# Fused adaLN, cached attention and token mixer at decode: epilogue pieces at two places of each round, and a tail with other engines

## The chip, the cores and the metric

The kernel runs on one NeuronCore of one Trainium2 chip. The metric is the device time of one execution in microseconds; shown are the median of the runs and, from one profiled execution, a trace. The engines are PE (TensorE: matrix products; PEld is its weight load), DVE (VectorE), ACT (ScalarE: activations from a table that has to be loaded), POOL (GpSimd) and SP (SyncE, which here only issues DMAs). Each engine works through its own instructions in the order in which they were written and waits on semaphores for the others.

## The reference

Four rows (B = 4) of width D = 512 go through an adaLN-conditioned block: attention with 32 query heads on 8 cached key/value heads of 4096 positions and 128 channels, and then a token-mixing MLP whose hidden width is F = 1792 (there is one token, so each of the 512 channels goes through the same small MLP 1 to 1792 to 1).

```python
mod = (_silu(c) @ w_mod).reshape(c.shape[0], 6, 1, -1)
sa, ca, ga, sb, cb, gb = (mod[:, 0], ..., mod[:, 5])
h = _layernorm(x, axis=-1) * (1 + ca) + sa
x = x + ga * _A_ref(h, A_k_cache, A_v_cache, A_wq, A_wo)
h = _layernorm(x, axis=-1) * (1 + cb) + sb
x = x + gb * _B_ref(h, B_w1, B_b1, B_w2, B_b2)

# _A_ref: p = softmax(q k^T / sqrt(128)); o = p v; return o @ wo
# _B_ref: h = layernorm(x); u = gelu(h * w1 + b1); return u @ w2 + b2
```

All is float32. The key and value caches are 2 x 32 tiles of 2 MB (one for each row and kv head), and w_q, w_o and w_mod add some 22 MB.

## The kernel before

A *round* i (0 to 31) is one pair of row b = i // 8 and kv head h = i % 8. The main loop runs rounds 0 to 27; rounds 28 to 31 are written out after it (the tail), and `finish` ends the last row. Five 2 MB buffers (`ring`) take K and V tiles in turn; SP issues each load when the buffer it takes has been read. The order on each engine is the order of the program: nothing is rescheduled.

One pass of the loop, number i, does in this order: the scores of round i + 2 (PE, L215) and their row maximum m (DVE, L218); the first half of the projection of round i - 1 (`project_a`, PE L292, then oT on DVE, L294); the transposes of the exponentials of round i + 1 (PE L245; copied to pT on DVE, L251); the second half of the projection (`project_b`, L303 or L310, added to acc on DVE, L319); `colmax` (PE L224, DVE L226) and `expo` (PE pb L233, DVE nm L235, ACT p L238, an Exp) of round i + 2, with the first half of the values product of round i (`values`, L267) between the two; the second half of the values; and the copy po of their result (DVE, L271).

When all 8 heads of row b are done, the *epilogue* of row b runs piece by piece in the eight rounds of the next row. `epilogue` (L394) is a generator, and the loop calls it after the second half of the values (L515 to L519), one piece a round and two in the fifth: (0) fold of the projections, residual and statistics; (1) adaLN (`gather`, `adaln`); (2) the second layernorm (`gather`, `bcast`, `affine`, whose hb is made by ACT at L374), and the first two *pairs*. A pair is two of the 14 blocks of the hidden width: `expand` makes it on DVE (L380), a Gelu activates it in place on ACT (L409, seven pairs to a row), and `contract` or, for rows 0 and 1, `contract_wide` reduces it on PE (L385, L391) into py. Then follow (3) contraction of pairs 0 and 1, pairs 2 and 3 made; (4) contraction of 2 and 3, pairs 4 and 5 made; (5) their contraction, pair 6 made; (6) its contraction, and ZK = py + b2 on DVE (L439). A pair is always contracted in a later piece than the one that made it, and a later round.

Row 2's epilogue runs in the loop only in rounds 24 to 27; its later pieces are called in the tail (L540, L551, L557) and in `finish` (L450, L452).

For the last row the attention gate is multiplied into the last two heads' output weights ahead of time: `spread_gate` makes the gate as a 128x512 tile, `fold_gate` (L487) multiplies it into eight 128x512 blocks of `wo` on DVE (L490). Four are done at the end of round 24 and four at the end of round 25 (L530). Round 30 projects with blocks 0 to 3, round 31 with 4 to 7.

`finish` (L442) has the last row's statistics, `modmm(pg, 5)` (the product for gb, 32 PE instructions, L200), adaLN, the remaining two pieces of row 2's epilogue, the second layernorm, and the last row's 14 blocks (DVE expansions L380, ACT L460 and L465, PE L385). After the expansions DVE multiplies rows 0 to 2 by gb and adds the residual (L467, L468), copies gb (L470), SP stores the three rows (L473), DVE finishes the last row (L474, L475), and ACT's queue stores it (L476).

Of the kernel before, what the change touches and what calls it, by code (L numbers as in the profile page):

```python
# [19 lines left out]
P = 128  # L20
# [11 lines left out]
def adaln_decode(ctx: ExitStack, tc: tile.TileContext, small, x, wmod, wq, kT, v, wo, out):  # L32
# [161 lines left out]
        if i == NS - 1:  # L194
            load_wm(5)

    def modmm(pm, t):
        for k in range(4):
            for c in range(4):
                mm(pm[32 * c:32 * c + 32, :], sT8[:, k].rearrange("p b r -> p (b r)"),  # L200
                   WM[t][:, k, c * P:(c + 1) * P], start=(k == 0), stop=(k == 3))
# [150 lines left out]
    def adaln(b, pst):  # L352
        mean, var = norm(pst)
        a = wk.tile([P, P], F32, name="a")
        h1 = wk.tile([P, P], F32, name="h1")
        r = rsqrt(var, P, "e", lambda: dv.scalar_tensor_tensor(
            a, XK[:, b], mean, prep[:, 3], op0=OP.subtract, op1=OP.mult))
        dv.scalar_tensor_tensor(h1, a, r, prep[:, 2], op0=OP.mult, op1=OP.add)
        return h1, stats(h1, b)

    def bcast(h1, b, pb=None):
        if pb is None:
            pb = ps_e.tile([P, 4, P], F32, name="phb", tag="e")
        for c in range(4):
            e = 32 * c + 8 * b
            mm(pb[:, c, :], ident[:, e:e + 1].to_broadcast([P, P]), h1, start=True, stop=True)
        return pb.rearrange("p c n -> p (c n)")

    def affine(pst, pb):
        mean, var = norm(pst)  # L370
        hb = wk.tile([P, D], F32, name="hb")
        wr = wk.tile([P, NF], F32, name="wr")

        nc.scalar.activation(hb, pb, AF.Identity, bias=mean, scale=-1.0)  # L374
        rsqrt(var, P, "e", out=wr, times=w1n)
        return hb, wr

    def expand(u, hb, wr, js):
        for e, j in enumerate(js):
            dv.tensor_scalar(u[:, e, :], hb, wr[:, j:j + 1], b1[:, j:j + 1], op0=OP.mult, op1=OP.add)  # L380
# [13 lines left out]
    def epilogue(b):  # L394
        residual(XK[:, b], fold_groups(ps_e, ACC.pop(b), "e"))
        stm = stats(XK[:, b], b)
        yield
        h1, stm = adaln(b, gather(stm))
        yield
        pst = gather(stm)  # L400
        hb, wr = affine(pst, bcast(h1, b))
        done = []

        def activate(*pairs):
            for j2 in pairs:
                js = (2 * j2, 2 * j2 + 1)
                u = up.tile([P, 2, D], F32, name="u")
                expand(u, hb, wr, js)
                nc.scalar.activation(u, u, AF.Gelu_apprx_tanh)  # L409
                done.append((u, js))  # L410

        activate(0, 1)
        yield
        wide = b < B - 2
        py = ps_e.tile([P, D if wide else P], F32, name="py", tag="e")

        def consume():
            while done:
                (contract_wide if wide else contract)(py, *done.pop(0))

        consume()
        activate(2, 3)
        yield
        consume()
        yield
        activate(4, 5)
        yield
        if wide:
            consume()
        activate(6)  # L430
        yield
        consume()
        if wide:
            yw = wk.tile([P, D], F32, name="yw", tag="yw", bufs=1)
            dv.tensor_copy(yw, py)
            py = fold_groups(ps_e, yw, "e")
        else:
            yield
        dv.tensor_scalar(ZK[:, b], py, b2, None, op0=OP.add)  # L439
        yield  # L440

    def finish(b, pg, xp, epi):  # L442
        uu = [ring.tile([P, 8, D], F32, name=f"uu{i}", tag="kv") for i in range(2)]
        U = [uu[j // 8][:, j % 8] for j in range(NF)]
        stm = stats(xp, b)
        dv.tensor_copy(XK[:, b], xp)
        pst = gather(stm)
        modmm(pg, 5)
        h1, stm = adaln(b, pst)
        next(epi)  # L450
        pst = gather(stm)
        next(epi)  # L452
        py = ps_s.tile([P, 8, P], F32, name="py3", tag="s")
        pb = bcast(h1, b, py[:, 4:])
        py = py[:, 0]
        hb, wr = affine(pst, pb)
        for js in ((0,), (1,), (2, 3), (4, 5), (6, 7), (8, 9), (10, 11), (12,), (13,)):
            j = js[0]
            if j < 2:
                nc.scalar.activation(U[j], hb, AF.Gelu_apprx_tanh, bias=b1[:, j:j + 1], scale=wr[:, j:j + 1])  # L460
                u = U[j].unsqueeze(1)
            else:
                u = uu[j // 8][:, j % 8:j % 8 + len(js)]
                expand(u, hb, wr, js)
                nc.scalar.activation(u, u, AF.Gelu_apprx_tanh)  # L465
            contract(py, u, js)
        dv.tensor_mul(osb[:, :B - 1], ZK, pg.unsqueeze(1).to_broadcast([P, B - 1, P]))  # L467
        dv.tensor_add(osb[:, :B - 1], osb[:, :B - 1], XK[:, :B - 1])  # L468
        gbl = cst.tile([P, P], F32, name="gbl")
        dv.tensor_copy(gbl, pg)  # L470
        dst = out.rearrange("b (c n) -> b c n", c=4)
        for e in range(B - 1):
            nc.sync.dma_start(dst[e], osb[8 * e:P:32, e])  # L473
        dv.scalar_tensor_tensor(osb[:, b], py, b2, gbl, op0=OP.add, op1=OP.mult)  # L474
        dv.tensor_add(osb[:, b], osb[:, b], XK[:, b])  # L475
        nc.scalar.dma_start(dst[b], osb[8 * b:P:32, b])  # L476

    def spread_gate():
        pgb = ps_m.tile([P, 4, P], F32, name="pgb", tag="m")
# [7 lines left out]
    def fold_gate(gate, es):  # L487
        for e in es:
            w = wo_t[HKV - 2 + e // REP][:, e % REP]
            dv.tensor_mul(w, w, gate)  # L490
# [6 lines left out]
        colmax(i)  # L497
        expo(i)
    transposes(0)
    epi = iter(())  # L500
    for i in range(NS - 4):
        load_k(i + 3)
        if i == NS - 5:
            load_k(NS - 1)
        load_v(i + 1)
        scores(i + 2)
        if i:
            project_a(i - 1)
        transposes(i + 1)
        if i:  # L510
            project_b(i - 1)
        colmax(i + 2)
        values(i, range(8))
        expo(i + 2)
        values(i, range(8, 16))  # L515
        if i and i % HKV == 0:
            epi = epilogue(i // HKV - 1)
        for _ in range((1, 1, 1, 1, 2, 1, 1, 0)[i % HKV]):
            next(epi, None)  # L519
        if 3 <= i <= 5:  # L520
            t = i - 1
            pm = mod(t)
            dst = prep[:, {2: 1, 3: 2, 4: 3}[t]]
            if t == 4:
# [5 lines left out]
        if i == NS - HKV or i == NS - HKV + 1:  # L530
            e = 4 * (i - NS + HKV)
            fold_gate(gate, range(e, e + 4))
    n = NS - 4
    load_v(n + 1)
    scores(n + 2)
# [1 line left out]
    transposes(n + 1)  # L537
    project_b(n - 1)
    colmax(n + 2)
    next(epi)  # L540
    expo(n + 2)
    scores(n + 3)
    transposes(n + 2)
    colmax(n + 3)
    expo(n + 3)
    values(n, range(16))
    load_v(n + 2)
    transposes(n + 3)
# [12 lines left out]
    values(n + 2, range(8, 16))  # L561
# [8 lines left out]
    mm(x3, ident, ep, start=False, stop=False)  # L570
    project_a(n + 3)
    project_b(n + 3, x3)
    finish(B - 1, pgx[:, 0], x3, epi)


# [29 lines left out]
```

## Time and profile before

| | |
|---|---|
| time, median of 3 runs | 392.44 us (392.14 to 392.52) |
| profiled execution | 395.09 us, of which the span of the trace is 393.3 us |
| mean granted TensorE clock | 0.904 |
| PE busy | 298.7 us (76%) |
| DVE busy | 180.7 us (46%) |
| ACT busy | 99.3 us (25%) |
| POOL busy | 0.7 us |
| HBM read | 157.32 MB, 400 GB/s over the span |

The times in the trace are microseconds from the start of the span. A row of the timeline has the start, the duration, the engine, the line of the kernel, the operation, the tiles (out<-in), the shapes and how many instructions were merged; in brackets stands how long the engine had been idle and what ended that. In the chain of waits a row has start, duration and the engine's work or transfer that the end of the kernel hung on.

### The profile page before, as it was taken

Reading aid. Unit: us, or ns where it says so; the run is one execution under the profiler, and the core shown is the slowest. Engines: PE = TensorE matmul, PEld = TensorE weight load, DVE = VectorE, ACT = ScalarE, POOL = GpSimd, SP = SyncE. Lnnn points to the kernel's source line nnn. Section 1 sums busy time; section 2 is a strip of 40 time slices with the busy share of each in tenths; the row PEclk is TensorE's granted clock in tenths of the full one; section 3 lists DMA queues with packets and bytes.
Section 4 is the critical chain, followed back from the end, with each engine's and each line's share of the span. In section 5 each row is a group of like instructions: output and inputs, shape, how many; then the busy total and the mean of one; then the engine's idle time right before and its main releaser. Section 6 shows DMA issues by size and latency. Waiting matters only on the chain.

```text
span 393.3 us, 7322 instructions
## 1 busy us (share of the span) xinstructions
PE 298.7 (76%) x3180; PEld 151.6 (39%) x3180; DVE 180.7 (46%) x491; ACT 99.3 (25%) x122; POOL 0.7 (0%) x6
## 2 busy tenths in 40 slices
PE   0576694837767478998788789888888777998976
PEld 0112342304324133453333345443334344565663
DVE  1522342304413232677454425675545357564465
ACT  1001211101101110116653202156541101474325
POOL 0000000000000000000000000000000000000000
PEclk9999588859969785999999969999999969899996
DMA  8999999999999999999999999999999999999600
GB/s 324 427 428 427 435 423 441 427 420 433 425 431 427 437 432 427 428 430 428 435 424 433 427 428 432 432 429 427 427 437 432 425 433 425 432 424 422 275 2 3
DMA packets 12711, 157.80 MB, mean 401 GB/s; under 512 B 1524, under 2 KB 1540, under 8 KB 1928
## 3 DMA queue, kind: packets, MB, share of 16 engines
q1 hardware_dynamic: 12672, 157.34, 94.1%
q8 instruction: 25, 0.41, 0.4%
q14 instruction: 6, 0.05, 0.0%
q10 hardware_dynamic: 8, 0.00, 0.0%
HBM read 157.32 MB, written 0.01 MB: 400 GB/s over the span
## 4 chain that ended last, share of the span: by engine, by line
DMA 53%; PE 35%; DVE 9%; ACT 1%; issue 1%; SPq 0%; DVEq 0%
DMA k<-in_kT 39%; DMA v<-in_v 12%; PE s L215 9%; PE pv L267 6%; PE s L245 3%; PE s L135 2%; PE py L385 2%; PE pq L310 2%; DMA sm<-in_small 2%; PE qs L150 2%; PE pt L292 2%; PE pa L303 2%; DVE m L218 2%; PE pb L233 1%; DVE mx L226 1%
## 5 line engine op out<-in xcount | busy, mean ns | idle before, releaser
L215 PE MATMUL s<-k,QT 128*32 128x512 f32 x512 | 73.8, 701 | 52.0 <-DMA k<-in_kT 51.7
L238 ACT ACTIVATE p<-s,nm 128x1024 f32<-128x1024 f32 x32 | 35.7, 1115 | 215.0 <-DVE nm L235 214.9
L218 DVE TENSOR_REDUCE m<-s 128x1 f32<-128x1024 f32 x32 | 39.2, 1224 | 90.8 <-PE s L215 90.7
L267 PE MATMUL pv<-v,pT 128*32 128x256 f32 x960 | 65.1, 390 | 5.0 <-DMA v<-in_v 4.8
L215 PEld LDWEIGHTS s<-k,QT 128*32 128x32 f32 x512 | 14.8, 119 | 86.9 <-DMA k<-in_kT 62.0
L245 PE MATMUL s<-ident,p 128*128 128x128 f32 x256 | 37.9, 296 | 0.0
L267 PEld LDWEIGHTS pv<-v,pT 128*32 128x32 f32 x960 | 26.8, 110 | 20.4 <-PE pm L224 5.3
L245 PEld LDWEIGHTS s<-ident,p 128*128 128x128 f32 x256 | 33.0, 162 | 2.3 <-ACT p L238 1.3
L292 PEld LDWEIGHTS pt<-sel,po 128*128 128x128 f32 x126 | 18.3, 209 | 30.7 <-issue 21.5
L303 PE MATMUL pa<-wo,oT 128*32 128x512 f32 x192 | 27.3, 642 | 0.0
L271 DVE COPY po<-pv 128x256 f32<-128x256 f32 x30 | 12.7, 425 | 26.3 <-PE pv L267 26.3
L409 ACT ACTIVATE u<-u 128x1024 f32<-128x1024 f32 x21 | 21.2, 1051 | 4.5 <-DVE u L380 4.4
L226 DVE TENSOR_REDUCE mx<-pm 1x128 f32<-1x512 f32 x32 | 21.5, 672 | 0.8 <-PE pm L224 0.8
L292 PE MATMUL pt<-sel,po 128*128 128x4 f32 x126 | 21.0, 272 | 0.5 <-DVE po L271 0.5
L380 DVE TENSOR_SCALAR u<-hb,wr,sm 128x512 f32<-128x512 f32 x42 | 20.2, 542 | 0.4
L319 DVE TENSOR_TENSOR acc<-acc,pa 128x512 f32<-128x512 f32 x21 | 14.4, 688 | 11.4 <-PE pa L303 11.4
L135 PE MATMUL s<-wm,sT 128*4 128x512 f32 x16 | 8.7, 702 | 14.0 <-DVE sT L121 14.0
L238 ACT ACT_TABLE_LOAD x10 | 12.8, 1283 | 19.7 <-DVE nm L235 19.6
L233 PEld LDWEIGHTS pb<-neg,mx 1*128 1x128 f32 x64 | 9.8, 190 | 17.3 <-DVE mx L226 16.1
L233 PE MATMUL pb<-neg,mx 1*128 1x1 f32 x64 | 12.5, 262 | 3.8 <-DVE mx L226 3.6
L409 ACT ACT_TABLE_LOAD x11 | 14.1, 1283 | 4.3 <-DVE u L380 4.2
L251 DVE COPY pT<-s 128x128 f32<-128x128 f32 x31 | 9.0, 291 | 11.5 <-PE s L245 11.0
(136 smaller groups left out, 229.5 us busy)
## 6 DMA issues: line engine op xcount, KB each, us to landing
k<-in_kT SPq DMA_DIRECT2D x32, 2048.0 KB, 21.8
v<-in_v SPq DMA_DIRECT2D x29, 2048.0 KB, 22.8
wq<-in_wq SPq DMA_DIRECT2D x4, 2048.0 KB, 17.7
wo<-in_wo SPq DMA_DIRECT2D x8, 1024.0 KB, 22.3
v<-in_v SPq DMA_DIRECT2D x5, 1024.0 KB, 15.6
wm<-in_wmod SPq DMA_DIRECT2D x2, 2048.0 KB
wm<-in_wmod SPq DMA_DIRECT2D x2, 1024.0 KB, 14.7
v<-in_v SPq DMA_DIRECT2D x1, 512.0 KB, 17.9
```

Source lines behind the costliest of these rows:

```text
L135: mm(s0[0:B, t * D:(t + 1) * D], sT[:, k, :], wm01[:, t, k, :], start=(k == 0), stop=(k == 3))
L215: mm(s[32 * c:32 * c + 32, n * 512:(n + 1) * 512], QT[:, b, h, :], KT[i][:, (n * 4 + c) * 512:(n * 4 + c + 1) * 512], start=True, stop=True)
L218: dv.tensor_reduce(m, s, axis=AX.X, op=OP.max)
L226: dv.tensor_reduce(mx, pm.rearrange("o (c r) -> o r c", c=4).unsqueeze(1).to_broadcast([1, 4, 32, 4]), axis=AX.X, op=OP.max)
L233: mm(pb, mx.rearrange("o c r -> o (c r)"), neg1, start=True, stop=True)
L238: nc.scalar.activation(p, s, AF.Exp, bias=nm, accum_out=l)
L245: nc.tensor.transpose(pt[:, k, :], p[:, k * P:(k + 1) * P], ident)
L267: mm(pv[32 * q:32 * q + 32, :], pTs[i % 3][:, k, :], VT[i][:, k * 2:(k + 1) * 2, :].rearrange("p j d -> p (j d)"), start=(k < 4), stop=(k ...
L292: mm(pt, po[:, c * DH:(c + 1) * DH], sel[:, c * REP:(c + 1) * REP], start=(c == 0), stop=(c == n - 1))
L303: mm(pa[32 * g:32 * g + 32, :], oT[:, g:g + 1].to_broadcast([P, 32]), wo_t[h][:, g, :], start=True, stop=True)
L380: dv.tensor_scalar(u[:, e, :], hb, wr[:, j:j + 1], b1[:, j:j + 1], op0=OP.mult, op1=OP.add)
L409: nc.scalar.activation(u, u, AF.Gelu_apprx_tanh)
```

## The change

The generator becomes a class `Mixer` whose pieces are called at two places of each round: the *inner* place, between `expo` and the second half of the values, and the *outer* place, where the generator was called. Residual, adaLN and second layernorm go to the inner place of the first three rounds of a row; pairs are made one by one, 0 at the outer place of the third round, then one at the inner and one at the outer place of the next rounds; at the outer place of rounds four to seven all pairs that are done are contracted, ahead of the new pair. ZK is made by ACT for row 2.

The gate products are spread: blocks 0 and 1 in round 24, 2 and 3 after the values of round 28, 4 and 5 around those of round 29, 6 and 7 after the projection of round 29. In the tail, pairs 3 to 6 of row 2 are made one at a time. In `finish` the gb product is split (k = 0 ahead of adaLN, k = 1 to 3 behind the broadcast), gb is copied before the last row's expansions, rows 0 to 2 are multiplied and added on GpSimd from that copy and stored by SP, and the last row's store is issued by SP too.

```diff
-    def modmm(pm, t):
-        for k in range(4):
+    def modmm(pm, t, ks=range(4)):
+        for k in ks:
...
+    class Mixer:
...
+        def inner(self, k):
+            if k == 0:
+                self.residual()
+            elif k == 1:
+                self.modulate()
+            elif k == 2:
+                self.normalise()
+            elif k <= 5:
+                self.both()
+
+        def outer(self, k):
+            if 3 <= k <= 6:
+                self.consume()
+            if 2 <= k <= 5:
+                self.both()
+            if k == 6:
+                self.close()
...
-        modmm(pg, 5)
+        modmm(pg, 5, (0,))
         h1, stm = adaln(b, pst)
-        next(epi)
+        mix.consume()
+        mix.close()
         pst = gather(stm)
-        next(epi)
         py = ps_s.tile([P, 8, P], F32, name="py3", tag="s")
         pb = bcast(h1, b, py[:, 4:])
         py = py[:, 0]
+        modmm(pg, 5, (1, 2, 3))
         hb, wr = affine(pst, pb)
+        gbl = cst.tile([P, P], F32, name="gbl")
+        dv.tensor_copy(gbl, pg)
+        po = nc.gpsimd
+        po.tensor_mul(osb[:, :B - 1], ZK, gbl.unsqueeze(1).to_broadcast([P, B - 1, P]))
+        po.tensor_add(osb[:, :B - 1], osb[:, :B - 1], XK[:, :B - 1])
+        dst = out.rearrange("b (c n) -> b c n", c=4)
+        for e in range(B - 1):
+            nc.sync.dma_start(dst[e], osb[8 * e:P:32, e])
...
-        dv.tensor_mul(osb[:, :B - 1], ZK, pg.unsqueeze(1).to_broadcast([P, B - 1, P]))
-        dv.tensor_add(osb[:, :B - 1], osb[:, :B - 1], XK[:, :B - 1])
-        gbl = cst.tile([P, P], F32, name="gbl")
-        dv.tensor_copy(gbl, pg)
-        dst = out.rearrange("b (c n) -> b c n", c=4)
-        for e in range(B - 1):
-            nc.sync.dma_start(dst[e], osb[8 * e:P:32, e])
         dv.scalar_tensor_tensor(osb[:, b], py, b2, gbl, op0=OP.add, op1=OP.mult)
         dv.tensor_add(osb[:, b], osb[:, b], XK[:, b])
-        nc.scalar.dma_start(dst[b], osb[8 * b:P:32, b])
+        nc.sync.dma_start(dst[b], osb[8 * b:P:32, b])
...
         expo(i + 2)
+        if i and i % HKV == 0:
+            mix = Mixer(i // HKV - 1)
+        if mix:
+            mix.inner(i % HKV)
+            if i == NS - HKV:
+                fold_gate(gate, (0, 1))
         values(i, range(8, 16))
-        if i and i % HKV == 0:
-            epi = epilogue(i // HKV - 1)
-        for _ in range((1, 1, 1, 1, 2, 1, 1, 0)[i % HKV]):
-            next(epi, None)
+        if mix:
+            mix.outer(i % HKV)
...
-    next(epi)
+    mix.consume()
     expo(n + 2)
+    mix.expand()
     scores(n + 3)
     transposes(n + 2)
     colmax(n + 3)
     expo(n + 3)
+    mix.gelu()
+    mix.both()
     values(n, range(16))
+    fold_gate(gate, (2, 3))
     load_v(n + 2)
     transposes(n + 3)
     project_a(n)
     project_b(n)
-    next(epi)
+    mix.both()
+    fold_gate(gate, (4,))
     values(n + 1, range(16))
     load_v(n + 3)
     pve = ps_s.tile([P, 2, 512], F32, name="pve", tag="s")
+    fold_gate(gate, (5,))
     values(n + 2, range(8), pve[:, 0, 0:2 * DH])
     project_a(n + 1)
-    next(epi)
+    mix.consume(1)
+    mix.both()
     project_b(n + 1)
+    fold_gate(gate, (6, 7))
     ep = cst.tile([P, P], F32, name="ep")
     residual(ep, ACC.pop(B - 1))
```

More of the change, by code (lines that the diff above doesn't have):

```diff
@@ L392, in contract_wide @@
                start=(j < 4), stop=(j >= NF - 4))
[L394 to L440, printed above, removed]
@@ L442, in finish, with __init__, residual, modulate @@
-    def finish(b, pg, xp, epi):
+    class Mixer:
+        def __init__(self, b):
+            self.b, self.wide, self.n = b, b < B - 2, 0
+            self.raw, self.done = [], []
+        def residual(self):
+            b = self.b
+            residual(XK[:, b], fold_groups(ps_e, ACC.pop(b), "e"))
+            self.st = stats(XK[:, b], b)
+        def modulate(self):
+            self.h1, self.st = adaln(self.b, gather(self.st))
+        def normalise(self):
+            self.hb, self.wr = affine(gather(self.st), bcast(self.h1, self.b))
+            self.py = None
+        def expand(self):
+            u = up.tile([P, 2, D], F32, name="u")
+            js = (2 * self.n, 2 * self.n + 1)
+            expand(u, self.hb, self.wr, js)
+            self.raw.append((u, js))
+            self.n += 1
+        def gelu(self):
+            u, js = self.raw.pop(0)
+            nc.scalar.activation(u, u, AF.Gelu_apprx_tanh)
+            self.done.append((u, js))
+        def both(self):
+            self.expand()
+            self.gelu()
+        def consume(self, most=9):
+            if self.py is None:
+                self.py = ps_e.tile([P, D if self.wide else P], F32, name="py", tag="e")
+            for u, js in self.done[:most]:
+                (contract_wide if self.wide else contract)(self.py, u, js)
+            del self.done[:most]
+        def close(self):
+            py = self.py
+            if self.wide:
+                yw = wk.tile([P, D], F32, name="yw", tag="yw", bufs=1)
+                dv.tensor_copy(yw, py)
+                py = fold_groups(ps_e, yw, "e")
+                dv.tensor_scalar(ZK[:, self.b], py, b2, None, op0=OP.add)
+            else:
+                nc.scalar.activation(ZK[:, self.b], py, AF.Identity, bias=b2)
+        def inner(self, k):
[14 more added lines that the diff above has]
+                self.close()
@@ L443, in finish @@
+    def finish(b, pg, xp, mix):
         uu = [ring.tile([P, 8, D], F32, name=f"uu{i}", tag="kv") for i in range(2)]
@@ L499, in adaln_decode @@
     transposes(0)
-    epi = iter(())
+    mix = None
     for i in range(NS - 4):
@@ L529, in adaln_decode @@
             gate = spread_gate()
-        if i == NS - HKV or i == NS - HKV + 1:
-            e = 4 * (i - NS + HKV)
-            fold_gate(gate, range(e, e + 4))
     n = NS - 4
@@ L572, in adaln_decode @@
     project_b(n + 3, x3)
-    finish(B - 1, pgx[:, 0], x3, epi)
+    finish(B - 1, pgx[:, 0], x3, mix)
 def kernel(**inputs):
```

## The prediction

> **What bounds the kernel now.** I read the page first (span, slices, transfers), then the chain of waits in order of time, then the timeline of the last 80 us, then the tables of busy time by stretch. The page:
>
> ```profile
> span 393.3 us, 7322 instructions
> DMA  8999999999999999999999999999999999999600
> k<-in_kT SPq DMA_DIRECT2D x32, 2048.0 KB, 21.8
> ```
>
> The 16 DMA engines are full until about 368 us. A K tile lands 21.8 us after its issue. At the slices' 427 GB/s its 2.1 MB take 4.9 us, so more than four transfers are queued, and a round of two tiles is 9.8 us long. Compute in the loop may run late by up to 21.8 - 4.9 = 17 us before a transfer starts late. So what the change does in the loop is free until the chain leaves the DMA for the last time:
>
> ```profile
> 293.66 23.00 DMA k<-in_kT
> 316.70 2.77 PE s L215 x16
> ...
> 332.63 1.14 DVE m L218
> 333.89 1.21 PE pq L310 x32
> ...
> 374.68 1.12 PE pgx L310 x32
> ...
> 390.14 0.29 DVE osb L475
> ```
>
> From 316.70 (scores 27) to the end the chain names no DMA any more (the lines left out are engines' too): 77 us in which every microsecond counts unless a load lands later. Two things held it in rounds 25 and 26. The second four gate products (L490) stand in DVE's queue ahead of the row maximum m (332.63), so TensorE had nothing to do until 333.89. And the clock:
>
> ```profile
> 310.77:314.19 3.42, 2.24 (x38) 1.38 (x42) 0.90 (x3) 0.57 (x1) 0.00 (x0) 1.00 0.98 422
> 314.19:317.60 3.41, 1.26 (x23) 0.40 (x19) 3.10 (x8) 0.64 (x2) 0.00 (x0) 1.00 1.03 442
> 317.60:324.43 6.83, 6.83 (x59) 4.55 (x51) 2.65 (x8) 0.00 (x0) 0.00 (x0) 0.50 1.00 427
> 331.24:334.65 3.41, 0.76 (x28) 0.76 (x32) 3.10 (x8) 0.00 (x0) 0.00 (x0) 1.00 1.02 437
> 334.65:338.06 3.41, 3.41 (x35) 1.43 (x31) 1.12 (x3) 0.00 (x0) 0.00 (x0) 0.51 1.01 432
> ```
>
> These are PE, PEld, DVE, ACT and POOL busy, granted clock, DMA share, GB/s. A stretch in which PE was busy for 1.26 or 0.76 of 3.41 us is followed by half clock; after one with 2.24 the clock stayed full.
>
> **Part 1: round 26, a gain of 4.1 us at scores 29.** The second quartet of gate products leaves round 25 (its row stands in part 4: 2.49 us), and the adaLN of batch 2 moves ahead of the second half of the values. The maximum of scores 28 can then start when those scores end, about 329.5, not 332.63, and PE goes on as soon as its transposes are through, about 331.2, not 333.89: 2.7 us. The stretch that called the half clock at 334.65 is then filled; 3.41 us at half clock that ran about 46% slower (scores 27 took 2.77, scores below 1.92) are worth 0.46 x 3.41 = 1.5. Scores 29 start near 340.52 - 4.1 = 336.4. Their K tile was issued at 314.39 and lands near 314.39 + 21.8 = 336.2, so no more can be had here.
>
> ```profile
> 314.39 0.33 SPq L181 DMA_DIRECT2D k<-in_kT  x1
> 340.52 1.92 PE L215 MATMUL s<-k,QT 128*32 128x512 f32 x16
> 344.52 1.08 PE L310 MATMUL pq<-wo,oT 128*32 128x128 f32 x32 [0.49 <-DVE oT L294]
> 346.74 0.38 PE L233 MATMUL pb<-neg,mx 1*128 1x1 f32 x2
> 347.39 1.28 ACT L238 ACT_TABLE_LOAD   x1 [2.75 <-DVE nm L235]
> 347.93 1.06 PE L385 MATMUL py<-u,sm 128*32 128x128 f32 x32
> 348.80 1.90 PE L215 MATMUL s<-k,QT 128*32 128x512 f32 x16
> 349.91 1.28 ACT L409 ACT_TABLE_LOAD   x1
> 351.20 2.00 ACT L409 ACTIVATE u<-u 128x1024 f32<-128x1024 f32 x2
> 353.22 1.28 ACT L238 ACT_TABLE_LOAD   x1
> ```
>
> **Part 2: round 27, a new wait that takes 3.4 us of it back.** Now the contraction at 347.93 reads pairs 0 and 1, activated a round earlier, and waits for nothing. After the change pair 0 is made at the outer place of round 26 and pair 1 at the inner place of round 27, and the outer place of round 27 contracts everything that is done, pair 1 too. PE thus stands at pair 1 until its Gelu has ended. Behind that Gelu, on ACT, stands the whole of exponential 29. Scores 29 to pb is 346.74 - 340.52 = 6.2 now; one pair expanded in DVE's way instead of two ends the 0.49 wait, 5.7. So pb 342.1, and ACT gets nm 0.65 later (347.39 - 346.74): 342.75. From there it needs, as the rows have it, 347.39 to 352.2 (load Exp, p with its read-out, load Gelu, one of the two Gelus, 1.0): 4.8. Pair 1 can be contracted from 347.6 or 347.7, and scores 30 follow 0.45 later: 348.15, against 348.80 now. PE has done the values and pair 0 by 343.8 and idles for 3.9 us; the gain is down to 0.65. The same wait comes in three rounds of each of batches 0 and 1, some 3 us each, and there the 17 us of queued transfers hide it; uncovered it would cost about 9 a batch. Bounds: if the Exp table is loaded before nm is ready, as at 353.22, scores 30 start at 346.9; the nearest row, the first Exp after a batch's first Gelus at 347.39, waited for nm, so I take 348.15.
>
> **Part 3: the clock after that wait.** A hole of 3.9 us leaves at least one stretch of 3.41 us with under half of it busy, whatever the phase, and 1.26 and 0.76 were enough above. I take one episode of 3.41 us in the rounds behind it. Its price lies between 0 (none) and 1.5 (part 1); two stretches, as at 317.60, would be 3.0. Some of the slow work hides behind DVE's maximum, which PE waits for anyway; I take 1.2. The Trainium skill ("TensorE: Matmul & The Clock Gate", HAM oscillation) asks for no PE gap above about 3.4 us; holes of 2.2 and 2.9 us sufficed in this trace, so the measurement is the stricter one, and by either this hole is long enough.
>
> **Part 4: the tail, 1.7 us more.**
>
> ```profile
> 330.14 2.49 DVE L490 TENSOR_TENSOR wo<-wo,gate 128x512 f32<-128x512 f32 x4
> 362.51 0.29 DVE L249 COPY pTl<-s 128x128 f32<-128x128 f32 x1 [0.64 <-PE s L245]
> 368.92 0.29 DVE L319 TENSOR_TENSOR acc<-acc,pq 128x128 f32<-128x128 f32 x1 [0.29 <-PE pq L310]
> 370.26 0.61 PE L292 MATMUL pt<-sel,po 128*128 128x4 f32 x4 [0.55 <-DVE po L271]
> ```
>
> Four products took 2.49: 0.62 each. Products 2 and 3 stand between the copy of values 28 and pTl. DVE had 0.64 idle there, so 1.2 of work costs about 0.5 (bounds 0 and 1.2), because oT and the projection come behind pTl. Products 4 and 5 hide: DVE expands one pair there instead of two (0.93 less) and waits for PE afterwards; without that cover, 1.2. Products 6 and 7 stand between acc at 368.92 and ep, and ep stands before the copy po for which the next PE group waits at 370.26: the full 1.2. The fourth Gelu of the tail sits on an idle ACT, and contracting pair 3 fills PE's wait for oT. Scores 30 to the end of the last projection is 374.68 + 1.12 - 348.80 = 27.0 now, 28.7 after. The last projection ends at 348.15 + 1.2 + 28.7 = 378.05 instead of 375.8: **+2.2**. No landing limits this: PE's chain named no load behind 316.70, and this tail runs later than that one.
>
> **Part 5: the finish, +0.1.**
>
> ```profile
> 1.01 0.29 POOL masks.py:199 TENSOR_SCALAR_AFFINE_SELECT ident<-ident 128x128 f32<-128x128 f32 x1
> 380.94 0.69 ACT L374 ACTIVATE hb<-py,mv 128x512 f32<-128x512 f32 x1 [11.15 <-PE py L366]
> 381.83 5.57 DVE L380 TENSOR_SCALAR uu<-hb,wr,sm 128x512 f32<-128x512 f32 x12 [0.30 <-ACT hb L374]
> 382.52 1.36 PE L385 MATMUL py<-uu,sm 128*32 128x128 f32 x16 [1.63 <-ACT uu L460]
> 383.08 5.87 ACT L465 ACTIVATE uu<-uu 128x1024 f32<-128x1024 f32 x7
> 388.48 1.73 SPq L473 DMA_DIRECT2D out<-osb  x3
> 390.47 1.11 ACTq L476 DMA_DIRECT2D out<-osb  x1
> ```
>
> Three quarters of the gb product go behind the broadcast, into PE's 1.63 wait; uncovered the 24 instructions would cost 0.8 (32 of the same shape take the 1.12 at 374.68). ZK's bias add goes to ACT's 11.15 of idleness and leaves DVE, where it stood in another wait: 0 both ways. The copy gbl (0.28) moves ahead of the 12 expansions, into DVE's 0.30 wait for hb: 0.1. The expansions come 0.93 a pair and ACT takes 0.97, with 0.4 us of slack at the first. The early rows' two DVE products leave the end, where DVE waited for PE: 0. On GpSimd each is 128x384; the only POOL row near it, 0.29 for 128 columns with one input, scales to 0.87. If they run beside DVE undisturbed they end before 385, the three stores are issued by 387, and the last store finds SP free. ACT issued its store the moment its data was ready, so SP gains nothing unless its 0.5 to 0.6 against 1.11 counts: -0.5 at best, and +1.7 if it queues behind the three. I take 0.
>
> **Sum.** Against its own span of 393.3 (run as a whole 395.09): -4.1 + 3.4 + 1.2 + 1.7 + 0.1 = **+2.3**, a span of 395.6. The runs' median is 392.44, so **394.7 us**. About 0.2%, 0.8 us, is what a measurement of this kernel tells from no change.
>
> **Rivals.**
>
> *Faster: the DVE queue was the cost, and the new wait is short.* If the Exp load before p29 doesn't wait for nm, pair 1 is ready 1.28 earlier, the hole is 2.6 us, and it may straddle two clock stretches. Scores 30 then start at 346.9 and the last projection ends at 346.9 + 28.7 = 375.6 instead of 375.8: -0.2. If products 2 and 3 also cost nothing (their lower bound in part 4, 0.5 less) and the SP store counts (0.5, part 5), the sum with the finish's 0.1 is -0.2 - 0.5 - 0.5 + 0.1 = -1.1: 391.3. It decides at the start of scores 30: at 347 or before, this case is open; from 347.6 on it can't come. For: round 26's gap is the largest in the chain. Against: in the first round of Gelus the load did wait.
>
> *GpSimd and DVE don't run together.* Twelve expansions follow one another without a hole, and ACT has 0.4 us of slack. If the two products take turns with them, 2 x 0.87 - 0.4 = 1.3 falls on ACT's stream; if they wait until the expansions end, they end 1.7 later, the three stores hold SP for 1.73, and the last store is about as late. Either way 396.0. No row before shows POOL beside DVE. The Trainium skill ("SBUF — State Buffer", SBUF: two separate sides) says a GpSimd operation and a two-port or two-input VectorE operation exclude each other for a whole instruction; no run here shows it yet.
>
> *The wait without the clock.* No half clock behind the hole: 393.5.
>
> *Nothing moves*, gain and wait cancel or the finish eats a gain: within 0.8 of 392.44.
>
> **Chances.** Forecast 0.30; GpSimd against DVE on top of it 0.20; the wait without the clock 0.10; the faster rival 0.24; nothing moves 0.16. Faster 0.24, same 0.16, slower 0.60. Range 391.3 (the faster rival) to 396.4 (the GpSimd rival and a little more); the forecast's own range is 393.5 to 395.7.
>
> **What would show it.** Part 1: scores 29 near 336.4, waiting for the load. Part 2: PE idle for 2.5 to 4 us in front of a contraction, ended by ACT's Gelu, in round 27 (and in rounds 11 to 13 and 19 to 21, where the DMA hides it). Part 3: a clock of 0.5 right behind it. Part 4: 1.2 us of gate products between acc and ep. Part 5: expansions still 5.6 us for 12. I am wrong if scores 30 start before 347, or if the finish from last projection to end differs from 17.5 by over 0.5.

## The result and the profile after

| | before | after |
|---|---|---|
| median of 6 runs each on one chip, us | 392.48 (392.14 to 394.14) | 403.9 (402.23 to 404.45) |
| ratio | | 1.0272, 95% interval 1.0243 to 1.0301 |
| profiled execution, us | 395.09 | 403.68 |

The change makes the kernel 11.4 us slower. The forecast said slower, by 2.3 us, and the range ended at 396.4; the time lies far outside it. Executions of one kernel here differ by 2 to 5 us (of 65 runs of the kernel before in the sets below, 23 took more than 394 us); so a profile is compared with a profile below, and medians with medians.

The page of the kernel after: span, DMA slices, the shares of the chain, and the K loads with their time from issue to landing.

```profile
span 401.9 us, 7320 instructions
DMA  8999999999999999999999999999999999998000
PE 45%; DMA 31%; DVE 13%; ACT 8%; issue 2%; SPq 0%; DVEq 0%; ACTq 0%
k<-in_kT SPq DMA_DIRECT2D x32, 2048.0 KB, 19.2
```

The DMA engines are as full as before until the last slices, so, as far as slices of 10 us show it, compute never let the queue run dry (a K tile still lands 19.2 us after its issue, where it was 21.8). All the same DMA carries only 31% of the chain. Where the chain leaves it is the main reading; these are rows of the chain of waits of the kernel after, in order of time (start, duration, engine, what):

```profile
162.31 20.78 DMA v<-in_v
183.23 1.07 PE pv L267 x16
184.88 1.28 ACT L238
186.17 1.20 ACT p L238 x2
187.40 1.28 ACT L422
188.69 1.06 ACT u L422
189.80 1.07 PE py L391 x2
190.88 0.84 PE py L391 x2
191.72 2.29 PE s L215 x14
...
282.99 1.06 ACT u L422
284.10 0.62 PE py L391 x2
285.26 3.30 PE s L215 x14
```

After 183.23 no load stands in the chain any more. From there to the end, 219 us, the time is set by compute, and in every round that contracts a fresh Gelu by the same sequence: p, Gelu table, Gelu, contraction, scores; in the first such round of each batch a load of the Exp table stands in front of p. The second view is the list of what PE waited for (total, times, longest), after:

```profile
PE s L215 <- DMA k<-in_kT: 25.2, 8, 6.4
PE py L391 <- ACT u L422: 17.4, 6, 3.4
PE py L385 <- ACT u L422: 3.8, 1, 3.8
```

Six times in batches 0 and 1 (L391) and once in batch 2 (L385) PE stood in front of a contraction for 2 to 3.8 us until ACT had made its Gelu. The same list for the kernel before, in a second profile that is told of below, has no such line and

```profile
PE s L215 <- DMA k<-in_kT: 47.4, 21, 6.4
```

The waits for K are 22.2 us shorter, and in their place stand 21.2 us (17.4 + 3.8) of waits for Gelus.

Behind the waits the clock falls. Windows of the kernel after (PE, PEld, DVE, ACT, POOL busy; granted clock; DMA share; GB/s):

```profile
198.00:208.00 10.00, 6.65 (x46) 2.18 (x46) 2.60 (x7) 7.06 (x7) 0.00 (x0) 0.83 1.00 427
278.00:288.00 10.00, 6.45 (x50) 1.83 (x42) 2.84 (x7) 7.06 (x7) 0.00 (x0) 0.84 1.02 437
346.34:349.75 3.41, 0.00 (x0) 0.00 (x0) 0.93 (x3) 3.37 (x5) 0.00 (x0) 1.00 1.00 423
349.75:353.16 3.41, 3.10 (x28) 1.38 (x32) 0.00 (x0) 1.20 (x2) 0.00 (x0) 0.50 0.99 423
360.00:363.41 3.41, 1.56 (x13) 1.35 (x13) 2.22 (x5) 0.67 (x2) 0.00 (x0) 1.00 1.01 419
363.41:366.82 3.41, 3.41 (x34) 1.46 (x33) 1.07 (x3) 2.90 (x4) 0.00 (x0) 0.50 1.02 423
```

In the two first, PE is busy for 6.5 of 10 us, with a clock of 0.83 and 0.84; the scores that follow such a wait took up to 3.30 us in the chain above, where they take 1.72 at full clock (at 297.82 of the same chain). The last four show two further episodes close to the end.

The steps that the prediction spoke of, in the timeline of the kernel after (start, duration, engine, line, operation; in brackets the idle time before and what ended it):

```profile
345.14 1.28 ACT L238 ACT_TABLE_LOAD   x1 [3.60 <-DVE nm L235]
350.06 1.08 PE L385 MATMUL py<-u,sm 128*32 128x128 f32 x16 [3.76 <-ACT u L422]
358.17 1.28 ACT L238 ACT_TABLE_LOAD   x1 [7.22 <-DVE nm L235]
360.73 1.09 PE L245 MATMUL s<-ident,p 128*128 128x128 f32 x8 [0.97 <-ACT p L238]
363.53 3.53 PE L267 MATMUL pv<-v,pT 128*32 128x256 f32 x32
388.33 0.69 ACT L374 ACTIVATE hb<-py,mv 128x512 f32<-128x512 f32 x1 [2.02 <-PE py L366]
389.16 0.29 DVE L481 COPY gbl<-pgx 128x128 f32<-128x128 f32 x1 [0.23 <-PE pgx L200]
389.60 1.00 POOL L483 TENSOR_TENSOR osb<-zk,gbl 128x384 f32<-128x384 f32 x1 [388.30 <-DVE gbl L481]
389.63 6.96 DVE L380 TENSOR_SCALAR uu<-hb,wr,sm 128x512 f32<-128x512 f32 x12 [0.18 <-DVE gbl L481]
390.68 1.06 POOL L484 TENSOR_TENSOR osb<-osb,xk 128x384 f32<-128x384 f32 x1
392.06 5.88 ACT L496 ACTIVATE uu<-uu 128x1024 f32<-128x1024 f32 x7 [1.48 <-DVE uu L380]
```

### The profile page after: what moved, and what is told of

It is laid out like the page before. It is cut to its first block, busy times and chain, and to the rows that moved or that the text cites. A ratio compares the mean times of both kernels' runs of the same rounds, so it can differ in the third digit from the quotient of the medians.

```text
span 401.9 us, 7320 instructions
## 1 busy us (share of the span) xinstructions
PE 311.4 (77%) x3180; PEld 153.5 (38%) x3180; DVE 179.9 (45%) x488; ACT 99.9 (25%) x123; POOL 2.8 (1%) x8
## 4 chain that ended last, share of the span: by engine, by line
PE 45%; DMA 31%; DVE 13%; ACT 8%; issue 2%; SPq 0%; DVEq 0%; ACTq 0%
DMA v<-in_v 17%; DMA k<-in_kT 12%; PE s L215 10%; PE pv L267 5%; PE s L245 5%; PE pa L303 4%; PE pt L292 3%; DVE mx L226 3%; PE py L391 2%; PE qs L150 2%; DVE acc L319 2%; PE s L135 2%; ACT p L238 2%; ACT L422 2%; PE pb L233 2%
## 5 line engine op out<-in xcount | busy, mean ns | idle before, releaser
L215 PE MATMUL s<-k,QT 128*32 128x512 f32 x512 | 84.5, 732 | 25.7 <-DMA k<-in_kT 25.2
L215 PEld LDWEIGHTS s<-k,QT 128*32 128x32 f32 x512 | 18.2, 126 | 64.1 <-issue 32.5
L391 PE MATMUL py<-u,sm 128*32 128x512 f32 x56 | 16.6, 674 | 17.4 <-ACT u L422 17.4
L303 PE MATMUL pa<-wo,oT 128*32 128x512 f32 x192 | 28.7, 673 | 0.0
## 6 DMA issues: line engine op xcount, KB each, us to landing
k<-in_kT SPq DMA_DIRECT2D x32, 2048.0 KB, 19.2
```

Source lines behind the costliest of these rows:

```text
L215: mm(s[32 * c:32 * c + 32, n * 512:(n + 1) * 512], QT[:, b, h, :], KT[i][:, (n * 4 + c) * 512:(n * 4 + c + 1) * 512], start=True, stop=True)
L303: mm(pa[32 * g:32 * g + 32, :], oT[:, g:g + 1].to_broadcast([P, 32]), wo_t[h][:, g, :], start=True, stop=True)
```

## The experiments

Ten kernels ran beside the kernel before, in three sets, each set on one chip, and the kernel before was profiled once more; the runs of the kernel before had a median of 392.9 us in the first set and the second, of 393.8 in the third. Ratios are against the runs of the same set; the change itself ran beside a median of 392.48, so a difference from its 403.9 us goes across sets.

**The kernel before, profiled again.** It belongs at the head, because it corrects the base of the forecast.

> The kernel before, unchanged, profiled a second time. Its first profiled execution took 2.65 us more than the median of its runs, and the trace shows half clock at 317.6 and again at 334.65. If the clock is what differs between executions, this one runs at another granted clock in rounds 25 and 26 and its span lies nearer to the median (about 390.7 us). If the 2.65 us are a cost of profiling itself, the span is again 393 us and the executions run as a whole 395.

It took 392.34 us, its span 390.5. In its chain of waits the last load is not at 316.70 but 30 us later:

```profile
324.28 21.76 DMA k<-in_kT
...
346.08 1.92 PE s L215 x16
```

and its timeline shows scores 29 and 30 waiting for K, although the gate products of round 25 still stand in DVE's queue:

```profile
327.44 2.49 DVE L490 TENSOR_TENSOR wo<-wo,gate 128x512 f32<-128x512 f32 x4
336.40 0.16 PEld L215 LDWEIGHTS s<-k,QT 128*32 128x32 f32 x8 [0.18 <-DMA k<-in_kT]
346.08 1.92 PE L215 MATMUL s<-k,QT 128*32 128x512 f32 x16 [1.28 <-DMA k<-in_kT]
349.04 1.28 ACT L238 ACT_TABLE_LOAD   x1
```

Scores 29 start at 336.40. This is the place (336.4) to which the prediction wanted to bring them from 340.52. So the 4.1 us belonged to that one execution, which ran parts of rounds 25 and 26 at half clock, and are no cost that every execution pays. (The last row, a load of the Exp table, is used further below.) The windows on the grid of the clock's stretches say why this one was spared:

```profile
312.12:315.53 3.41, 2.60 (x42) 1.46 (x42) 1.06 (x4) 1.21 (x2) 0.00 (x0) 1.00 0.98 418
315.53:318.95 3.42, 2.04 (x18) 0.61 (x18) 2.94 (x8) 0.00 (x0) 0.00 (x0) 1.00 1.04 446
318.95:322.36 3.41, 3.20 (x59) 2.70 (x62) 2.71 (x7) 0.00 (x0) 0.00 (x0) 1.00 0.99 423
```

PE has the same hole of about 2.2 us in front of scores 27 here, but it falls across a border of two stretches, PE is busy for 2.60 and 2.04 us of them, and the clock stays full.

**The ledger against this profile.** Starts of scores, in us, from the timelines (the column "later" is after less before):

| scores | before (second profile) | after | later | contraction one call later (below) |
|---|---|---|---|---|
| 17 | 218.26 | 227.63 | 9.4 | 219.47 |
| 21 | 257.71 | 258.68 | 1.0 | 258.36 |
| 22 | 266.85 | 270.14 | 3.3 | 269.03 |
| 23 | 276.67 | 284.11 | 7.4 | 278.71 |
| 24 | 286.35 | 296.79 | 10.4 | 288.39 |
| 25 | 296.74 | 307.98 | 11.2 | 298.84 |
| 27 | 316.91 | 322.37 | 5.5 | 317.68 |
| 29 | 336.40 | 338.86 | 2.5 | 337.15 |
| 30 | 346.08 | 350.91 | 4.8 | 346.83 |
| 31 | 352.05 | 357.83 | 5.8 | 352.80 |

A round with no Gelu takes 7.3 us after the change (scores 26 to 27: 315.08 to 322.37, 7.29), a K and V tile come every 9.7: so the lag shrinks by about 2.4 a round, but the rounds with Gelus take 11 to 14 us. The three waits of batch 0 made 9.4 us of lag at scores 17, of which 1.0 was left at scores 21; the three of batch 1 made 11.2 at scores 25, and at scores 29, after four rounds, 2.5 are left. From there: round 29 itself 2.4, scores 30 to 31 1.0 more, scores 31 to pb 31 1.0 more (5.36 against 4.39), pb 31 to the end of the last projection 3.2 more, the finish 1.4 more (18.7 against 17.3). The sum, 11.4, is the difference of the two spans, 401.9 - 390.5. The experiments take it apart.

**The contraction one call later.** The newest pair is left for the next call, so that PE never stands behind a Gelu of the same round.

```diff
         def outer(self, k):
-            if 3 <= k <= 6:
+            if 3 <= k <= 5:
+                self.consume(len(self.done) - 1)
+            if k == 6:
                 self.consume()
```

> The changed kernel, but at the outer place a pair is contracted one call later (the newest pair that is done is left for the next round), so that PE never waits for a Gelu of its own round. Theory 'the wait for the fresh Gelu, and what it leaves behind': the loop's lag (scores 25 were 11 us late), the 3.8 us hole of round 27 and the half clocks behind it go; scores 29 start at 336.4 and scores 30 at about 346 as their loads land; with the tail's gate products, the Exp load ahead of p30 and the GpSimd finish left in, 396 to 397 us. Rival 'the loop's lag is covered by the DMA queue': only round 27's hole and one half clock go, about 399.5 us.

397.01 us (396.27 to 398.28), ratio 1.0101 (1.0065 to 1.0136): 6.9 us of the 11.4 are gone. Its list of PE's waits has lost both lines for u, and the K loads have their place back:

```profile
PE s L215 <- DMA k<-in_kT: 62.2, 26, 8.1
```

Scores 30 wait for K again and start at 346.83, scores 29 at 337.15.

**The same in batches 0 and 1 alone.** The rounds of batch 2 keep the wait; this asks what the early waits cost at the end.

```diff
-            if 3 <= k <= 6:
+            if 3 <= k <= 5 and self.wide:
+                self.consume(len(self.done) - 1)
+            elif 3 <= k <= 6:
                 self.consume()
```

> The same later contraction, but for rows 0 and 1 alone, whose epilogues run in rounds 8 to 23; row 2's stays as in the changed kernel. Theory 'lag': the loop's lag reaches the tail, scores 29 go from 338.9 to about 336.4, time 2.5 us less than the changed kernel (about 401.4). Rival 'covered': no difference from the changed kernel's 403.9.

401.83 us (400.75 to 404.52), ratio 1.0228 (1.0179 to 1.0277). Scores 29 wait for their load again:

```profile
337.99 1.92 PE L215 MATMUL s<-k,QT 128*32 128x512 f32 x16 [0.81 <-DMA k<-in_kT]
349.50 0.64 PE L385 MATMUL py<-u,sm 128*32 128x128 f32 x16 [3.76 <-ACT u L422]
```

So the early waits alone are what brings compute behind the loads at scores 29. Their price is about 2.1 us by the medians, though the interval of the ratio overlaps with the one after the change. The profiles differ by 2.1 us too, but only 0.9 of it is the lag (scores 29 at 337.99 against 338.86; the loads themselves land later in this execution than in the second profile, where scores 29 start at 336.40). The rest comes at scores 30, which ran at full clock here (1.90 us) and partly at half clock after the change (3.02), behind the same wait. The one wait that is left, 3.76 us in round 27, makes most of the difference to the experiment before this one, 4.8 us by the medians, 4.6 by the spans: 0.8 stand already at scores 29, 2.3 come at scores 30 (11.97 from scores 29, where the other has 9.68), and 1.5 behind it, where values 28 run at half clock.

**The early rows' products back on VectorE,** behind the expansions, with the three stores behind them; all else as after the change.

```diff
-        po = nc.gpsimd
-        po.tensor_mul(osb[:, :B - 1], ZK, ...)
-        po.tensor_add(osb[:, :B - 1], osb[:, :B - 1], XK[:, :B - 1])
...
             contract(py, u, js)
+        dv.tensor_mul(osb[:, :B - 1], ZK, ...)
+        dv.tensor_add(osb[:, :B - 1], osb[:, :B - 1], XK[:, :B - 1])
...
```

> The changed kernel, but the early rows' product and sum go back from GpSimd to DVE, behind the last row's expansions (the copy gbl stays ahead of them, the last store stays on SP). Theory 'GpSimd and DVE take turns': the 12 expansions go from 6.96 us back to 5.6 and the time falls by 1.3 to 1.5 (about 402.5). Rival 'something else delays the expansions' (the copy gbl, the later hb): 403.9, expansions still near 7 us.

402.69 us (400.84 to 403.01), ratio 1.023 (1.0191 to 1.027), 1.2 less than after the change, inside what either median moves by; the profile is clearer. Its expansions:

```profile
390.04 5.57 DVE L380 TENSOR_SCALAR uu<-hb,wr,sm 128x512 f32<-128x512 f32 x12 [0.18 <-DVE gbl L481]
```

5.57 us as before, where they took 6.96 beside GpSimd.

**The kernel before with those products on GpSimd,** the counterpart: gbl is copied ahead of the expansions, and GpSimd works beside them.

> The kernel before, with only this part of the change: gbl copied ahead of the expansions, the early rows' product and sum on GpSimd. Theory 'take turns': expansions about 7 us, time 392.5 + 1.4 = 393.9. Rival: no difference from before, 392.5; a third way, the stores of the early rows are early and free SP: below 392.5.

394.64 us (393.46 to 397.67), ratio 1.0028 (0.9993 to 1.0063): by the time alone it can't be told from no change. The timeline has the same two signs, expansions of 6.96 us and ACT waiting for them:

```profile
381.36 1.00 POOL L460 TENSOR_TENSOR osb<-zk,gbl 128x384 f32<-128x384 f32 x1 [380.06 <-DVE gbl L458]
381.38 6.96 DVE L380 TENSOR_SCALAR uu<-hb,wr,sm 128x512 f32<-128x512 f32 x12
383.81 5.88 ACT L473 ACTIVATE uu<-uu 128x1024 f32<-128x1024 f32 x7 [1.09 <-DVE uu L380]
```

**The gate products in the loop.** On top of the later contraction: two products at the end of each of rounds 24 to 27, none in the tail.

```diff
             mix.outer(i % HKV)
+            if i >= NS - HKV:
+                e = 2 * (i - NS + HKV)
+                fold_gate(gate, (e, e + 1))
...
-    fold_gate(gate, (2, 3))
...
-    fold_gate(gate, (6, 7))
```

> The later contraction of the experiment before (397.0 us), and the eight gate products two per round at the end of rounds 24 to 27, none in the tail. If the tail's gate products cost the 0.5 and 1.2 us that the prediction gave them, 395.3 us, and the stretch from the end of values 29 to the end of the last projection is 1.2 us shorter. Rival: the products push the row maxima of rounds 24 to 27 back and TensorE waits there instead: scores 31 start later by 0.6 us or more and the time stays at 397.

396.17 us (394.96 to 398.87), ratio 1.0076 (1.0044 to 1.0109). In the profiles pb 31 to the end of the last projection falls from 18.34 us (358.16 to 376.50) to 16.77 (357.44 to 374.21), the 1.6 us that the tail's products cost; scores 31 don't come later (352.07 against 352.80). The rival is out; that the medians show 0.8 and not 1.6 lies within their spread.

**The Exp table early.** On top of the later contraction: an exponential of one element right behind the Gelus.

```diff
             mix.outer(i % HKV)
+            if 2 <= i % HKV <= 5:
+                nc.scalar.activation(warm, ones[0:1, 0:1], AF.Exp)
```

> The later contraction (397.0 us), and a one-element exponential right behind the Gelu of rounds 2 to 5 of each batch, so that the table of the exponential is loaded while ACT is idle and not behind the wait for the row's maximum. If the load of 1.28 us on the way from nm to p sets the pace in rounds 26 to 28, each of these rounds and the first of the tail ends up to 1.3 us sooner and the time is 396.0 (395 at best). Rival: the row maxima on VectorE and the loads of K set the pace there, the load hides behind them: 397.0.

397.53 us (396.49 to 398.21), ratio 1.0092 (1.0058 to 1.0126): no gain in the time. In the profile the term is there: scores 31 to pb 31 take 4.39 us (352.26 to 356.65), as before the change, and not 5.36. But this execution met a half clock in the tail:

```profile
366.96:370.37 3.41, 1.68 (x32) 1.10 (x28) 2.61 (x8) 1.06 (x1) 0.00 (x0) 1.00 0.76 305
370.37:373.78 3.41, 3.41 (x72) 3.40 (x68) 0.00 (x0) 0.00 (x0) 0.00 (x0) 0.50 0.35 144
```

Whether the shorter way to pb 31 makes such an episode likelier or this was chance, one trace can't say: it stays open.

**All four together.** Later contraction, gate products in the loop, early Exp table, early rows' products on VectorE.

> Four edits on the change: the later contraction, the gate products two per round in the loop, the early load of the exponential's table, and the early rows' two products back on VectorE. If the four gains add up (6.9, 1.7, 1.0 and 1.2 us off 403.9), 393.1 us, the same as before within half a us. Rival: they share one slack, since with the later contraction the loads of K end the wait in rounds 26 to 30 again, and the sum stays at 394.5 or above.

393.68 us (392.79 to 396.39), ratio 1.0013 (0.998 to 1.0046): the four edits take back the whole loss, within that interval. The profiled execution took 395.01 us, 1.3 above the median; its windows and its chain show a half clock on the path:

```profile
343.47:346.89 3.42, 1.47 (x36) 0.84 (x32) 3.38 (x7) 3.32 (x4) 0.00 (x0) 1.00 1.06 455
346.89:350.30 3.41, 3.41 (x18) 0.74 (x10) 0.19 (x1) 2.65 (x4) 0.00 (x0) 0.50 0.96 404
```

```profile
346.63 3.44 PE s L216 x16
```

Scores 30 at half clock cost 3.44 - 1.92 = 1.5 us on the path.

**The finish as before.** On the last one: the copy gbl behind the expansions, the last store on ACT's queue.

> The kernel with the four edits (393.7 us median; 392.8 to 393.0 in half its runs), with the copy gbl behind the twelve expansions and the last store on ACT's queue, as they are before the change. In its profile the first paired Gelu starts 2.33 us after hb, before the change 2.15, and the last store is issued 0.34 us after its data is ready only because SP is just through with three others (388.54 + 1.73 = 390.27). If both are costs, 0.2 + 0.3 = 0.5 us less: 393.2 us median. Rival: they lie beside the landing of the store, 393.7.

392.62 us (392.34 to 394.58), ratio 0.9978 (0.9954 to 1.0002). The edge that the change put on the finish is gone: from the last projection's end to the end of the span 17.3 us (373.09 to 390.4), as before. The interval reaches 1, so it is the kernel before over again, no gain.

**The first contraction of the tail moved** behind the maximum of scores 31.

```diff
     colmax(n + 2)
-    mix.consume()
     expo(n + 2)
     mix.expand()
     scores(n + 3)
     transposes(n + 2)
     colmax(n + 3)
+    mix.consume()
```

> The same, and the first contraction of the tail moved from in front of pb 30 to behind the maximum of scores 31, where TensorE waits 0.85 us for the row maximum before pb 31. If this contraction (1.01 us in the chain) stands on the way from the last K load to the end, scores 31 start 1.0 sooner, pb 31 0.85 sooner, and the time is 392.3 us, at or below the kernel before. Rival: transposes 30 then wait for p 30, or the last V pieces land too late: no change, 393.2.

392.66 us (392.33 to 395.37), ratio 0.9985 (0.9959 to 1.001): neither came. The wait moved instead, to pb 30:

```profile
352.39 0.38 PE L234 MATMUL pb<-neg,mx 1*128 1x1 f32 x2 [0.80 <-DVE mx L227]
```

Scores 30 to 31 take 5.83 us and not 4.97: without the contraction PE waits 0.80 us for DVE's maximum there. The chain named the contraction with 1.01 us, but DVE's branch beside it is only 0.2 shorter. Taking work off one branch of a join brings only the distance to the other. In this execution, 1.7 us above the median, PE also waits 0.91 us for V 30 (at 365.02), which the profile of the kernel before it in this list does not; so the rival's late V pieces were met here, and whether they cost the median run anything stays open.

**The first part of the change alone.** The kernel before, gate products two per round in rounds 24 to 27.

```diff
-        if i == NS - HKV or i == NS - HKV + 1:
-            e = 4 * (i - NS + HKV)
-            fold_gate(gate, range(e, e + 4))
+        if i >= NS - HKV:
+            e = 2 * (i - NS + HKV)
+            fold_gate(gate, (e, e + 1))
```

> The kernel before with one part of the change alone: the gate products two per round in rounds 24 to 27 instead of four in rounds 24 and 25. The prediction gave this part 4.1 us (388.3 us). The second profile of the kernel before says that scores 29 wait for their K load anyhow, at 336.4, when the clock is full: then the median stays at 392.6, and at most the executions with half clock in rounds 25 and 26 get fewer.

393.3 us (392.1 to 395.75), ratio 0.9999 (0.9968 to 1.003). The 4.1 us are not there, and the runs reach as high as those of the kernel before in this set (392.02 to 395.87): nothing shows that the half clock in rounds 25 and 26 became rarer either.

## Why the prediction was wrong, step by step

**The base: "-4.1 at scores 29".** Wrong. It was read from one execution, 2.65 us above the median, whose half clocks at 317.60 and 334.65 were taken as part of the kernel; the sum made against that span was then carried to the median, which had never paid these 4.1 us. The second profile (scores 29 at 336.40, waiting for K) and the first part run alone (ratio 0.9999) show it. (The 1.5 us for a stretch of 3.41 at half clock is about right, but scores 27 don't give it: their 2.77 us began with 0.9 at full clock. Scores that ran almost wholly at half clock took 3.44 in the run with all four edits, 1.5 more than 1.92.) Against the second profile the prediction's own terms would have given 348.15 - 346.08 = 2.1 at scores 30, then 1.2 + 1.7 + 0.1, 5.1 us in all and not 2.3.

**"What the change does in the loop is free until the chain leaves the DMA for the last time."** This is the step that failed in its reasoning. The 17 us of queued transfers keep the transfers from starting late, and they did: the DMA slices stay at nine tenths to the end of the loads. But they don't bring compute back. A lag is gone only when PE again waits for a load, and about 2.4 us a round is what a round without Gelus gains on the loads. The prediction had priced these waits well ("about 9 a batch"; the lag was 9.4 us behind batch 0 and grew by 10.3 in batch 1) and then hid them whole. The rounds behind batch 0 did hide 8.4 us; the four between batch 1 and scores 29 hid 8.7 of 11.2 and left 2.5, and the chain left the DMA at 183, not at 316. Shown by the contraction one call later, which brings the K waits back, and by the same in batches 0 and 1 alone, where scores 29 wait for K again; there the gain at scores 29 is 0.9 and not 2.5 us, because the loads land later in that execution.

**Part 2, the wait for the fresh Gelu.** Right in mechanism and size: forecast 3.9 us of idleness in front of a contraction in round 27, measured 3.76; also the six in the earlier rounds (2.0 to 3.35). ACT's Exp load waited for nm (3.60), as taken. Scores 30 came 4.8 later than in the second profile: 2.5 of lag and 2.4 of this wait; the prediction's 348.15 against 346.08 is 2.1.

**Part 3, the clock behind it.** Right in kind, too small in number: one episode of 1.2 was taken, "two stretches, as at 317.60, would be 3.0" stood in the bounds. Two came near the end: scores 30 (1.0 more to scores 31) and values 28 (3.53 where the profile before has 1.93: 1.6). The second follows the stretch that holds PE's wait for p 30. The first need not come: with the later contraction in batches 0 and 1 alone, scores 30 ran at full clock behind the same wait of 3.76 us.

**Left out: the Exp load ahead of p 30.** Gelus stand between the exponentials of rounds 29 and 30 in both kernels. Before the change the Exp table behind them is loaded at once (349.04 in the second profile, 353.22 in the first), before nm 30 is there; after it the load waits 7.22 us, until nm is there (358.17), and its 1.28 us come on the way to p. The prediction had weighed both cases for round 27 and didn't ask it for round 30. pb 30 to transposes 30 is 1.0 longer, T 30 waits 0.97 for p. The early Exp table takes just that away (4.39 against 5.36), though not the time of that kernel. What decides whether such a load goes ahead of nm no run here shows: in the kernel before as in the one after, some do and some don't.

**Part 4, the tail's gate products: 1.7.** Right: 1.6 by the two profiles with and without them.

**Part 5, the finish: 0.1.** Wrong, 1.4: the finish is 18.7 us long, and a distance of over 0.5 from 17.5 had been named as a sign of being wrong. Two parts. GpSimd's products and the expansions disturb each other: 6.96 against 5.57 us, ACT waits 1.48 for its first pair; this rival had stood there with 1.3 and a chance of 0.2. And two edits that were costed at 0.1 and at nothing meet: gbl was moved ahead of the expansions, the last three quarters of gb behind the broadcast, so the copy gbl waits for PE (389.16) and the expansions start 1.30 us after hb (388.33 to 389.63), where before it was 0.90 (378.37 to 379.27). Of these 0.4 us 0.2 reach ACT: its first pair starts 2.33 us after hb with the products on VectorE, 2.15 before the change; the rest of the 1.4 is GpSimd's. The SP store, put at nothing: right. When the products ran on VectorE it queued behind the three others, as the prediction feared, but by some 0.3 and not 1.7.

**What was missed.** Of 11.4 - 2.3 = 9.1 us, 2.8 are the base (5.1 - 2.3), the largest part. The rest, against the second profile, is 11.4 - 5.1 = 6.3 us. Of it 2.5 are the lag at scores 29 (0.9 by the run that takes it away alone), 0.3 more in round 29, 1.4 the clock (1.0 + 1.6 - 1.2), 1.0 the Exp load, 1.3 the finish, less 0.1 for the gate products: 6.4.

## What to carry to other kernels

Slack in a DMA queue protects the transfers, not the end: ask for each stage whether compute still waits for a load after it, and how many us a round it can catch up, before a stall there is called free. Profile the kernel before twice, and take the execution at the median, before a gain is read out of a gap; a stretch of half clock that one execution meets and another does not can look like a defect in the order of the work. A contraction of a value that another engine makes in the same round belongs one call later: that alone was worth 6.9 us here.

## What the runs showed of the hardware

**The clock is granted on a fixed grid of 3.41 us, and what counts is PE's busy time in a stretch, not the length of one hole.** All thirteen traces, laid on this grid, have stretches at full or at half clock as a whole, nothing between. From 42 us to 10 us before the end they hold 1075 stretches at full clock. Of these 77 had PE busy for under 1.48 us, and half clock followed 75 of them; it followed 37 of the 139 with 1.48 to 2.12 us, and 3 of the 859 above that (some matmul records can be missing, which makes the border soft). The same hole of 2.2 us in front of scores 27 led to 6.83 us of half clock in the first profile and to none in the second; on the grid it left 1.26 us of work in one stretch there, and 2.60 and 2.04 in two here. The Trainium skill ("TensorE: Matmul & The Clock Gate", HAM oscillation) warns of PE gaps above about 3.4 us; in front of 363.41 two shorter ones in one stretch, the waits of 0.97 us for p 30 and of 1.13 for the row maximum, were enough, so the measurement is the stricter one.

**GpSimd beside VectorE.** Two GpSimd products of 1.00 and 1.06 us (128x384, two inputs each) stretched the twelve expansions beside them by 1.39 us, less than the 2.06 that they took. On VectorE the same two take 0.56 each. The Trainium skill ("SBUF — State Buffer", SBUF: two separate sides) tells of a port that the two share, held by one of them for a whole instruction; the traces agree that they hinder each other, but what the expansions lost is two thirds of GpSimd's time and not all of it.
